# An attention front end with routed experts: the first group's v load put behind k, its queries turned early, the second group's loads issued early, the third group's casts in other buffers

## Chip, cores, metric

The kernel runs on one core of one Trainium2 chip. The metric is device time in microseconds (us) of one execution. Several executions are timed, in rounds that alternate with the kernel before on the same chip. A ratio is the mean time of one kernel's fast runs over the mean of the other's fast runs of the same rounds, so it is not quite the ratio of the medians quoted beside it. "Fast" leaves out the executions over 1.5% above the fastest of the same kernel.

## The reference

Attention in which a query sees only keys of its own hash bucket (six sign bits of a projection), then a gated mixture of eight experts over the result.

```python
q_bits = (einsum('bhsd,dk->bhsk', q, proj) > 0); k_bits = likewise with k
mask = q_bucket == k_bucket                      # buckets from the six bits
attn = softmax(where(mask, q @ k.T / sqrt(64), -1e9)) @ v   # B, H, S, D = 4, 8, 768, 64
x = attn, as 3072 x 512
P = exp(x @ w_gate), then 8 rounds of row and column normalisation
out = sum over 8 experts e of P[:, e] * (relu(x @ w1[e]) @ w2[e])
```

## The kernel before

The attention goes in 8 groups of four heads (two groups a batch). The code below is condensed, with cuts marked by `...`. A group has 24 "units" (4 heads x 6 key tiles). A unit is a pair of score matmuls `st` on TensorE, one `exp` on ScalarE, and six small `num` matmuls. While group n is computed, `prepare(n + 1)` runs in steps that are tied to units by `due`: transposes on VectorE (DVE), casts on GpSimd (POOL), hash matmuls `pr`, bits, and many small copies that SyncE (SP) issues. From the third group on, spare TensorE time goes to the first expert's matmuls (`hp`, `yp`), so TensorE is nearly full from there (busy for 10.00 of the 10 us from 70 to 80).

```python
    def fetch(n, what, eng=nc.gpsimd):       # k, q: 768 KB each, v: 4 x 192 KB
        ...
    def prepare(n):
        ...                                  # t16: casts of k and q
            if n == 0:
                if x == 0:
                    t16 = hpool.tile([P, FO, S], F16, tag="h", name="t16")
                t16s[name] = t16[:, 2 * x:2 * x + 2, :]
            else:
                t16s[name] = wk.tile([P, 2, S], F16, tag="t16", name="t16")
        ...
        lag = 2 if n > 2 else 1
        due = (4, 5, 8, 9, 12, 15) if n == 1 else (0, lag, 2 * lag, 3 * lag, 4 + 3 * lag, 7 + 3 * lag)
        yield due[0]; turn_qk("k", 0)        # transpose (DVE) and cast (POOL)
        yield due[1]; turn_qk("k", 1); stack("k", 0)      # copies by SP, two a head
        if n == 0:
            for c in range(2): hashed("k", c)             # PE, into PSUM tile pr
            bits("k")                                     # DVE, from pr
        if n: stack("k", 1); fetch(n + 1, "k")
        yield due[2]; turn_qk("q", 0)
        yield due[3]; turn_qk("q", 1); stack("q", 0)
        if n: stack("q", 1); fetch(n, "v")
        ...                                  # weight loads of 1 MB for n = 2, 3, 5, 6
        yield due[4]; ...                    # n == 0: hashed("q"), bits("q"); else all hashes and bits
        if n < 3:
            move_bits("k"); move_bits("q")   # head 0: bits straight to ks, qs
        put_bits()                           # all bits to DRAM (ds<-bt)
        ...
        yield due[5]
        ...                                  # get_bits of heads 1 to 3 from DRAM, rest of the stacks
        cast_v()                             # POOL: 2 casts, then 6 sums
        if n == 0:
            fetch(1, "kq")
    ...
    fetch(0, "kqv", nc.sync)
    pin(nc.scalar.activation(out=mark, in_=ones[:, 0:1], func=Act.Exp))
    for x in range(32):                      # warm-up matmuls
        if x == 10:
            for _ in prepare(0): pass
        pin(nc.tensor.matmul(warm, ident, vas[1]..., start=True, stop=True))
```

The softmax here doesn't subtract the row's maximum and nothing guards it: scores larger than these inputs give would overflow.

Of the kernel before, what the change touches and what calls it, by code (L numbers as in the profile page):

```python
# [20 lines left out]
def kernel(  # L21
# [11 lines left out]
    nc = tc.nc  # L33
# [28 lines left out]
    def pin(ins):  # L62
        tc.keep_in_program_order(ins)
        return ins
# [11 lines left out]
    mark = consts.tile([P, 1], F32)  # L76
# [270 lines left out]
    nat, grp = {}, {}  # L347

    def fetch(n, what, eng=nc.gpsimd):
        b, g = groups[n]  # L350
        for name, src in (("k", k), ("q", q)):
            if name in what:
                x = 12 if name == "k" else 15
                t = acc_flat[:, x * DD:(x + 3) * DD].rearrange("p (m d) -> p m d", d=D)
                pin(eng.dma_start(out=t, in_=src[b, g * HG:(g + 1) * HG].rearrange("h (r m) d -> (h r) m d", r=R)))
                nat[name, n] = t
        if "v" in what:
            t = lv.tile([P, HG, KT * D], F32, tag="v", name="v")
            vsrc = v[b, g * HG:(g + 1) * HG].rearrange("h (r m j) d -> m r h (j d)", r=R, m=M4)
            for m in range(M4):  # L360
                pin(eng.dma_start(out=t[R * m:R * (m + 1)], in_=vsrc[m]))
            nat["v", n] = t

    def prepare(n):
# [4 lines left out]
        for x, name in enumerate("kq"):  # L369
            trs[name] = acc_flat[:, (18 + 3 * x) * DD:(21 + 3 * x) * DD].rearrange("p (c t) -> p c t", c=2)  # L370
            d[name] = wk.tile([P, HG, S], F16, tag=name + "s", name=name + "s")
            if n == 0:
                if x == 0:
                    t16 = hpool.tile([P, FO, S], F16, tag="h", name="t16")
                t16s[name] = t16[:, 2 * x:2 * x + 2, :]
            else:
                t16s[name] = wk.tile([P, 2, S], F16, tag="t16", name="t16")
# [20 lines left out]
        def hashed(name, c):  # L398
            o = 64 * "kq".index(name)
            for x in range(2):  # L400
                pin(nc.tensor.matmul(d["pr"][o + 32 * x:o + 32 * (x + 1), 0:HT], pb[:, c].rearrange("p a r -> p (a r)"),  # L401
                                     trs[name][:, c, x * HT:(x + 1) * HT], start=(c == 0), stop=(c == 1)))

        def bits(name):
            if name == "k":
                d["bt"] = wk.tile([P, HT], F16, tag="bt", name="bt", bufs=1)
            bt, pr = d["bt"], d["pr"][:, 0:HT]
            if name == "k":
                pin(nc.vector.tensor_scalar(bt[0:64], pr[0:64], 0.0, 0.5, op0=Alu.is_gt, op1=Alu.subtract))
                pin(nc.vector.tensor_scalar(bt[0:64], bt[0:64], BIG, None, op0=Alu.mult))  # L410
            else:
                pin(nc.vector.tensor_scalar(bt[64:P], pr[64:P], 0.0, qoff[64:P, 0:1], op0=Alu.is_gt, op1=Alu.subtract))
# [15 lines left out]
        def cast_v():  # L428
            v32 = wk.tile([P, 2, 3, D], F32, tag="v32", name="v32", bufs=1)
            for i in range(2):  # L430
                hs = slice(2 * i, 2 * i + 2)
                pin(nc.gpsimd.tensor_copy(va[:, hs, :, 0:D],
                                          nat["v", n][:, hs, :].rearrange("p h (t d) -> p h t d", d=D)))
            for i in range(2):
                hs = slice(2 * i, 2 * i + 2)
                pin(nc.gpsimd.tensor_tensor(v32, va[:, hs, 0:3, 0:D], va[:, hs, 3:6, 0:D], op=Alu.add))
                pin(nc.gpsimd.tensor_tensor(v32[:, :, 0], v32[:, :, 0], v32[:, :, 1], op=Alu.add))
                pin(nc.gpsimd.tensor_tensor(vs[:, hs, 0:D], v32[:, :, 0], v32[:, :, 2], op=Alu.add))

        lag = 2 if n > 2 else 1  # L440
        due = (4, 5, 8, 9, 12, 15) if n == 1 else (0, lag, 2 * lag, 3 * lag, 4 + 3 * lag, 7 + 3 * lag)
        yield due[0]
        turn_qk("k", 0)
        yield due[1]
# [3 lines left out]
        if n == 0:  # L448
            for c in range(2):
                hashed("k", c)  # L450
            bits("k")
        if n:
            stack("k", 1)
            if n + 1 < len(groups):
# [17 lines left out]
        if n == 0:  # L472
            for c in range(2):
                hashed("q", c)
            bits("q")
        else:
            d["pr"] = ops.tile([P, 512], F32, tag="o", name="pr")
            for c in range(2):
                for name in "kq":
                    hashed(name, c)  # L480
                if c == 0 and n < 3:
                    yield due[4] + 1
            bits("k")
            bits("q")
# [25 lines left out]
        if n:  # L510
            get_bits("k", 3)
            get_bits("q", 3)
        cast_v()
        if n == 0:
            fetch(1, "kq")

    def scores(n, h, kt):
        d = grp[n]
# [89 lines left out]
        for _ in it:  # L608
            pass

    fetch(0, "kqv", nc.sync)
    pin(nc.scalar.activation(out=mark, in_=ones[:, 0:1], func=Act.Exp))
    warm = ops.tile([P, 512], F32, tag="o", name="warm")
    for x in range(32):
        if x == 10:
            for _ in prepare(0):
                pass
        pin(nc.tensor.matmul(warm, ident, vas[1].rearrange("p h t d -> p (h t d)")[:, 0:512],
                             start=True, stop=True))
# [8 lines left out]
    due = 0  # L628
    owed = 0.0
    for u in range(len(units) + 1):  # L630
        if u < len(units):
            n, h, kt = units[u]
            b, g = groups[n]
            i = u % per
            if i == 0:
                prep = prepare(n + 1) if n + 1 < len(groups) else iter(())
                due = 0
            while due is not None and due <= i:
                due = next(prep, None)
            if n == len(groups) - 1 and i == 2:  # L640
                for _ in quarters_of_w(1):
                    pass
                for _ in quarters_of_w2(1):
                    pass
            if u + 1 < len(units):
                pts[u + 1] = scores(*units[u + 1])
# [216 lines left out]
```

## Time and profile before

Median 784.56 us of three runs (783.94 to 786.2). The execution that was profiled took 786.34 us.

The page's second part, the whole span in 40 slices of about 20 us: busy tenths of TensorE (PE), and the clock that it was granted.

```profile
PE   6888999999999999999999999999999999999996
PEclk9997999999999999999999999999999999999999
```

TensorE is busy for 90% or more from the fifth slice on. The clock digit drops to 7 in the fourth (about 59 to 79 us). So most of what can be won without less matmul work lies in the first four slices. The timeline of TensorE there (start, duration, instruction, shape, count, and in brackets the idle time before it with what ended it):

```profile
13.15 4.92 PE L618 MATMUL warm<-va,ident 128*128 128x512 f16 x22
17.91 0.81 PE L521 MATMUL st<-qs,ks 71*128 71x384 f16 x4
...
59.32 0.66 PE L521 MATMUL st<-qs,ks 71*128 71x384 f16 x2 [1.14 <-ACT pt L524]
...
66.50 0.80 PE L521 MATMUL st<-qs,ks 71*128 71x384 f16 x2 [2.60 <-DMA qs<-ds]
69.74 1.44 PE L583 MATMUL hp<-xT,t 128*128 128x384 f16 x4 [0.30 <-ACT pexp L569]
...
76.14 0.81 PE L583 MATMUL hp<-xT,t 128*128 128x384 f16 x4
```

The first scores follow the warm-up matmuls at 17.91. At 66.50 TensorE has waited 2.60 us for the bits of the third group's second head. Four `hp` matmuls then take 1.44 us, later 0.81 (the last overlaps what follows). The stretches by window (start:end, length, busy us of PE, PEld, DVE, ACT, POOL with counts, granted clock, DMA share, GB/s) give the clock:

```profile
60.00:70.00 10.00, 6.73 (x94) 4.73 (x91) 5.67 (x10) 6.34 (x9) 5.75 (x10) 0.78 0.60 170
70.00:80.00 10.00, 10.00 (x77) 5.20 (x76) 4.68 (x10) 3.24 (x4) 4.20 (x7) 0.71 1.04 235
```

The chain of waits, followed back from the end of this part, runs through those bits (start, length, what):

```profile
55.69 5.88 DMA ds<-bt
61.91 4.45 DMA qs<-ds
66.50 0.80 PE st L521 x2
```

The put-bits copy to DRAM takes 5.88 us to land and the get-bits copy 4.45. ScalarE's timeline has the first exps:

```profile
18.43 8.73 ACT L524 ACTIVATE pt<-st 128x768 f16<-128x768 f32 x12 [16.14 <-DMA qs<-t]
```

| read from the timelines of this execution | us |
|---|---|
| first exp | 18.43 |
| 48 units at ScalarE's pace (0.73 us) | 35 |
| the same 48 units, from score pair to score pair | 41.4 |
| TensorE waits at units 24, 48, 54 | 1.04, 1.14, 2.60 |
| 60th exp (units counted from 0) | 80.07 |

### The profile page before, as it was taken

What the parts mean: (1) busy time and instruction counts of PE and PEld (TensorE: products, weight loads), DVE (VectorE), ACT (ScalarE), POOL (GpSimd) and SP (SyncE); (2) the same over time, 40 slices, a digit from 0 to 9 for tenths busy, and PEclk for the clock granted to TensorE, in tenths of its full rate; (3) what the DMA queues carried; (4) which work ended last, traced back from release to release, by engine and by line L of the source; (5) the groups of instructions that cost most, each with busy time, mean ns of one, the idle gap of its engine ahead of it and who ended that gap; (6) DMA issues with size and microseconds to landing.
All of it is one profiled execution on the core that took longest, in us unless ns stands there. A gap on an engine that the chain in (4) does not pass through costs nothing.

```text
span 784.6 us, 16637 instructions
## 1 busy us (share of the span) xinstructions
PE 751.7 (96%) x6252; PEld 518.2 (66%) x6252; DVE 558.1 (71%) x1240; ACT 507.7 (65%) x1020; POOL 312.6 (40%) x314
## 2 busy tenths in 40 slices
PE   6888999999999999999999999999999999999996
PEld 2554656666655667777777777777777777777663
DVE  3554757766758877777777777777777777777774
ACT  1894767777754777766666666666666666666660
POOL 6555355537600133344434334333444443324220
PEclk9997999999999999999999999999999999999999
DMA  5968467463003364486468647764874496443335
GB/s 151 252 153 203 118 168 156 143 156 89 2 1 55 54 108 81 83 160 108 82 110 158 109 81 131 129 118 82 147 121 92 92 168 108 81 82 81 81 82 135
DMA packets 42131, 88.56 MB, mean 113 GB/s; under 512 B 7426, under 2 KB 22402, under 8 KB 42050
## 3 DMA queue, kind: packets, MB, share of 16 engines
q0 software_dynamic: 27440, 71.06, 46.4%
q1 hardware_dynamic: 13718, 15.45, 7.5%
q10 hardware_dynamic: 892, 0.99, 0.5%
q8 instruction: 49, 0.80, 0.4%
q14 instruction: 32, 0.26, 0.1%
HBM read 53.07 MB, written 7.08 MB: 77 GB/s over the span
## 4 chain that ended last, share of the span: by engine, by line
PE 81%; DVE 5%; ACT 5%; DMA 3%; issue 2%; POOL 2%; SPq 2%; ACTq 0%; POOLq 0%; DVEq 0%
PE a L741 18%; PE a L249 17%; PE d L741 13%; PE y L249 9%; PE st L521 5%; PE d L249 4%; PE hp L583 4%; PE yp L593 3%; PE num L537 3%; ACT pt L524 2%; PE hp L322 1%; DMA ds<-bt 1%; ACT acc L240 1%; PE yp L306 1%; PE pr L401 1%
## 5 line engine op out<-in xcount | busy, mean ns | idle before, releaser
L750 DVE CUSTOM_DVE_ANT_0 hT<-d,u 128x384 f16<-128x384 f32 x336 | 185.1, 551 | 96.3 <-ACT u L746 95.6
L253 ACT ACTIVATE vt<-a,p 128x256 f32<-128x256 f32 x324 | 153.3, 473 | 149.2 <-PE a L249 148.9
L524 ACT ACTIVATE pt<-st 128x768 f16<-128x768 f32 x192 | 146.7, 809 | 69.2 <-PE st L521 52.4
L746 ACT COPY u<-a 128x384 f32<-128x384 f32 x336 | 160.9, 479 | 23.3 <-PE a L741 19.7
L288 POOL DMA_DIRECT2D acc<-vt x72 | 61.4, 852 | 267.9 <-ACT vt L253 112.4
L249 PEld LDWEIGHTS <-hT 128*128 128x128 f16 x1296 | 126.3, 97 | 50.7 <-DVE hT L750 1.1
L249 PE MATMUL a<-t,hs 128*128 128x256 f16 x972 | 145.8, 273 | 2.0 <-ACT vt L253 1.0
L249 PEld LDWEIGHTS <-hs 128*128 128x128 f16 x972 | 94.8, 98 | 38.3 <-issue 2.8
L741 PEld LDWEIGHTS <-t 128*128 128x128 f16 x896 | 87.7, 98 | 36.4 <-issue 0.6
L741 PE MATMUL d<-xd,t 128*128 128x384 f16 x448 | 109.4, 326 | 0.3 <-DVE hT L750 0.3
L741 PE MATMUL a<-xT,s 128*128 128x384 f16 x448 | 109.4, 326 | 0.1
L521 PE MATMUL st<-qs,ks 71*128 71x384 f16 x384 | 95.3, 329 | 10.7 <-ACT pt L524 5.6
L249 PE MATMUL y<-t,hT 128*128 128x256 f16 x648 | 97.1, 272 | 0.0
L257 DVE SCALAR_TENSOR_TENSOR acc<-y,p,acc 128x256 f32<-128x256 f32 x162 | 77.3, 477 | 11.4 <-PE y L249 11.4
L537 PEld LDWEIGHTS <-pt 128*128 128x128 f16 x1152 | 61.2, 98 | 27.3 <-issue 1.8
L741 PEld LDWEIGHTS <-s 128*128 128x128 f16 x672 | 65.5, 98 | 17.3 <-issue 2.3
L537 PE MATMUL num<-va,pt 128*128 128x65 f16 x1152 | 67.3, 195 | 0.6 <-ACT pt L524 0.6
L521 PEld LDWEIGHTS <-ks 71*128 71x128 f16 x384 | 33.8, 99 | 34.6 <-issue 17.2
L780 ACT ACTIVATE hT<-a 128x384 f16<-128x384 f32 x112 | 54.0, 483 | 1.8 <-PE a L741 1.7
L741 PE MATMUL a<-xd,s 128*128 128x384 f16 x224 | 54.3, 323 | 0.7 <-ACT u L746 0.6
L741 PE MATMUL d<-xT,t 128*128 128x384 f16 x224 | 54.7, 326 | 0.0
L741 PE MATMUL a<-xT,t 128*128 128x384 f16 x224 | 54.7, 326 | 0.0
(102 smaller groups left out, 969.7 us busy)
## 6 DMA issues: line engine op xcount, KB each, us to landing
acc<-vt POOLq DMA_DIRECT2D x72, 512.0 KB, 4.8
t<-in_moe_w_dram POOLq DMA_DIRECT2D x24, 512.0 KB, 7.3
acc<-in_k_dram POOLq DMA_DIRECT2D x7, 768.0 KB, 5.7
acc<-in_q_dram POOLq DMA_DIRECT2D x7, 768.0 KB, 12.4
v<-in_v_dram POOLq DMA_DIRECT2D x28, 192.0 KB, 5.5
out_dram<-acc SPq DMA_DIRECT2D x82, 64.0 KB
t<-in_moe_w_dram POOLq DMA_DIRECT2D x4, 1024.0 KB, 11.5
ks<-t SPq DMA_DIRECT2D x64, 48.0 KB
```

What stands on the lines that cost most here:

```text
L249: pin(nc.tensor.matmul(dst, hq[hn][:, fo, :], wq[wn][:, fo, :], start=first and fo == 0, stop=fo == FH - 1, skip_group_check=True))
L253: pin(nc.scalar.activation(out=vt[:, k], in_=a, func=Act.Copy, scale=p))
L257: pin(nc.vector.scalar_tensor_tensor(out=dst, in0=src, scalar=p, in1=dst, op0=Alu.mult, op1=Alu.add))
L288: pin(nc.gpsimd.dma_start(out=acc[:, b, i], in_=vt, accum_op=Alu.add))
L521: pin(nc.tensor.matmul(st[:, i, 0:HT], d["k"][0:KR, h, kt * P:(kt + 1) * P], d["q"][0:KR, h, i * HT:(i + 1) * HT], start=True, stop=True))
L524: pin(nc.scalar.activation(out=pt, in_=st[:, :, 0:HT], func=Act.Exp, scale=scale))
L537: pin(nc.tensor.matmul(num[:, j * (D + 1):(j + 1) * (D + 1)], pf[:, j * P:(j + 1) * P], va[:, h, kt, :], start=(kt == 0 and j == 0), stop= ...
L583: pin(nc.tensor.matmul(hp[:, 0:HT], w1[:, do, fo * P:(fo + 1) * P], xT[:, do, b * S + t * HT:b * S + (t + 1) * HT], start=(do == 0), stop= ...
L741: pin(nc.tensor.matmul(bk, wq[wn][:, do, f * P:(f + 1) * P], xq[xn][:, do, :], start=first and do == 0, stop=do == 1, skip_group_check=True))
L746: pin(nc.scalar.copy(t, bk))
L750: pin(add(TENSOR_ADD_SAT, out=dst, in0=bk, in1=u, s0=3e38, s1=0.0))
L780: pin(nc.scalar.activation(out=hT[:, f, hi], in_=a, func=Act.Relu))
```

## The change

The intent is a shorter front: let q arrive before v and turn it at once; fetch the second group's k and q before V's sums rather than after them, with its steps one or two units sooner; and free the third group from the two t16 buffers, which the second group's copies still read.

```diff
@@ prepare
-            if n == 0:
+            if n in (0, 2):                      # third group's casts in an h buffer
@@ cast_v
                 pin(nc.gpsimd.tensor_copy(va[:, hs, :, 0:D], ...))
+            if n == 0:
+                fetch(1, "kq")                   # between V's casts and V's sums
             for i in range(2): ...               # sums
@@ prepare
-        due = (4, 5, 8, 9, 12, 15) if n == 1 else ...
+        due = (3, 4, 7, 8, 10, 13) if n == 1 else ...
@@
             for c in range(2):
                 hashed("k", c)
-            bits("k")
@@
             for c in range(2):
                 hashed("q", c)
+            bits("k")                            # behind the queries' hash matmuls
             bits("q")
@@
         cast_v()
-        if n == 0:
-            fetch(1, "kq")
@@ start
-    fetch(0, "kqv", nc.sync)
+    fetch(0, "kq", nc.sync)
     pin(nc.scalar.activation(out=mark, in_=ones[:, 0:1], func=Act.Exp))
+    pin(nc.scalar.copy(mark, nat["k", 0][:, 0, 0:1]))    # waits for k
+    fetch(0, "v", nc.scalar)
```

More of the change, by code (lines that the diff above doesn't have):

```diff
@@ L440, in prepare @@
         lag = 2 if n > 2 else 1
-        due = (4, 5, 8, 9, 12, 15) if n == 1 else (0, lag, 2 * lag, 3 * lag, 4 + 3 * lag, 7 + 3 * lag)
+        due = (3, 4, 7, 8, 10, 13) if n == 1 else (0, lag, 2 * lag, 3 * lag, 4 + 3 * lag, 7 + 3 * lag)
         yield due[0]
```

## The prediction

> **What bounds the kernel now.** From about 76 us on, TensorE: the stretches by window show it 100% busy at full clock. No changed line touches that part; it can only begin sooner. What is left to win is the front:
>
> - 0 to 17.9 us, start: in the timeline the first score matmul (17.91) follows the last warm-up matmul (22 of them, 4.9 us, behind the queries' hash matmuls at 11.52 to 13.2).
> - 17.9 to 59.3 us, 48 score units: ScalarE's exp sets the pace, 0.73 us from start to start, 35 us for 48; they take 41.4. ScalarE's timeline shows 8.8 us of idle up to 67.4: 2.4 around 27 to 31 (third head's first unit, hash matmuls), 0.9 at 38.6 (a DMA), 1.3 at 45 to 48 (hash matmuls), 1.2 at 59 (third group's first head), 2.8 before 67.4 (third group's second head: TensorE waits 2.6 for the get-bits DMA).
> - 66.5 to 75.5 us: after that wait the clock is about half: four hp matmuls take 1.44 us instead of 0.65; granted clock 0.78 and 0.71 in 60:70 and 70:80. [...] I read this as about 4 us lost.
>
> **What the change moves.** It adds one small `mark` copy (0.2 us); v's four issues move from SP to ScalarE, idle then.
>
> 1. q no longer shares bandwidth with v, so its transposes (1.8 us) follow k's at 8.4 instead of 10.5; k's bits come 0.5 us later, q's 2 us sooner. The 22 warm-up matmuls then end near 16, and so does the wait for q's bits: 2 us saved. v should still land near 11, when GpSimd needs it.
> 2. The second group's k and q are issued near 13 instead of 18.5, so their transposes come at 19 to 22 instead of 23.7 to 29; with bits two units earlier this preparation gains 4 us (then limited by SP's issues, 0.6 to 0.7 us each). That takes most of the 24th unit's wait and 1 us of the 27 to 31 gap. Its 1.5 MB now meets the first group's small copies at 14 to 19: up to 1 us of new wait at the first group's second head.
> 3. The third group's casts no longer wait for the second group's copies out of the t16 buffers (k's 1.4 us at 43.8, q's at 49.1). Casts, bits and put-bits come 8 us sooner (put-bits now: issue 55.7, landing 5.9 later, then 4.5 for get-bits: the chain of waits from 45 to 66.5). The waits at 59 and 66.5 shrink to under 1 us together, and the cold clock goes.
>
> **Sum** (an estimate from these): 2.0 start, 1.3 at unit 12, 0.6 at unit 24, 1.0 and 2.4 in group three, 4.0 cold clock, less 1.0 of new waits: 10.3 us, all on the critical path, since what follows is TensorE bound. The ideal is about 15, so over 2% (15.7) is unlikely.
>
> Predicted 774.0 us, 80% range 770.0 to 780.0. Chances: faster by over 2% 0.05, within 2% 0.94, slower 0.01.
>
> **What would show it.** First score matmul near 16; the second group's k transposes before 20; no TensorE wait over 1.5 us between 17 and 66; granted clock 1.0 in 50 to 80; the gate matmuls (lg) at 60 to 62 instead of 68.6; from there equal timelines, shifted.
>
> **What would make it wrong.** The first group's bits through DRAM are delayed by the early loads (several us at unit 6); one remaining idle still drops the clock; SP's issues, not buffers, hold the third group; or the first unit still waits for q's bits near 17.5.

## The result, and the profile after

Median 783.7 us (783.4 to 783.73, 4 runs) against 784.25 for the kernel before (783.66 to 786.2, 4 runs); ratio 0.9988, 95% interval 0.997 to 1.0006. The change has no measurable effect. The prediction, 774.0 with a range of 770 to 780, was wrong.

The page's second part after the change:

```profile
PE   6999999999999999999999999999999999999996
PEclk9699999999999999999999999999999999999999
```

The clock is now full in the fourth slice and low in the second. The timeline of TensorE, the lines that answer to those of before:

```profile
8.83 2.40 PE L401 MATMUL pr<-acc,pb 128*32 128x384 f32 x16
11.17 4.92 PE L620 MATMUL warm<-va,ident 128*128 128x512 f16 x22
15.93 0.33 PE L521 MATMUL st<-qs,ks 71*128 71x384 f16 x1
20.75 1.12 PE L521 MATMUL st<-qs,ks 71*128 71x384 f16 x3 [4.50 <-DMA qs<-bt]
22.13 0.80 PE L521 MATMUL st<-qs,ks 71*128 71x384 f16 x2 [0.26 <-ACT pt L524]
...
69.61 0.81 PE L583 MATMUL hp<-xT,t 128*128 128x384 f16 x4 [0.30 <-ACT pexp L569]
```

The warm-up matmuls do end near 16, as predicted, and q, loaded without v beside it, does come sooner: VectorE's four transposes of k and q run from 6.43 to 10.23 without a gap, where q's two began at 10.50 before. But the second half of the first score pair waits 4.50 us for q's bits, and the matmuls after it run slow (a score pair 0.80 instead of 0.48). So the first exp comes at 21.27:

```profile
21.27 1.51 ACT L524 ACTIVATE pt<-st 128x768 f16<-128x768 f32 x2 [14.58 <-PE st L521]
```

At the other end, the wait of 2.60 us is gone and `hp` runs at full speed; it starts at 69.61, where it started at 69.74. The wait did not go because the bits come sooner. The third group's put-bits and the get-bits for the queries of its second head are issued 2.3 and 2.5 us later than before (55.69 and 61.91 there):

```profile
58.02 0.44 SPq L417 DMA_DIRECT2D ds<-bt  x1
64.36 0.42 SPq L420 DMA_DIRECT2D qs<-ds  x1
```

It went because the units come later: exp 48 is at 63.36, where it was at 60.08. The stretches by window:

```profile
20.00:30.00 10.00, 8.99 (x67) 5.51 (x67) 3.04 (x6) 7.18 (x9) 2.17 (x3) 0.52 0.61 169
30.00:40.00 10.00, 9.45 (x101) 5.24 (x99) 5.51 (x10) 7.20 (x10) 5.70 (x9) 0.80 0.81 167
60.00:70.00 10.00, 9.10 (x130) 6.43 (x129) 7.81 (x14) 9.52 (x14) 9.05 (x14) 1.00 0.76 200
```

The low clock has moved from 66 to 76 us forward to 20 to 34. The chain of waits at the start, and the issues by GpSimd and ScalarE just before (POOL's timeline, then ACT's), show what held the bits:

```profile
12.99 1.99 DMA ks<-bt
15.01 5.70 DMA qs<-bt
```

```profile
14.47 0.74 POOL L355 DMA_DIRECT2D acc<-in_k_dram  x1
15.20 0.57 POOL L355 DMA_DIRECT2D acc<-in_q_dram  x1
```

```profile
12.81 2.94 ACTq L426 DMA_DIRECT2D qs<-bt  x2
```

The second copy of q's bits (5.2 KB) goes out at 15.01, when the copy of k's bits has landed, and lands at 20.70. The second group's k and q (1.5 MB) were issued at 14.47 and 15.20. The DMA view of the 2 us from 16 to 18 (queue, packets, MB, share of the 16 engines) has one queue only, GpSimd's:

```profile
q0 software_dynamic: 95, 0.58, 88.1%
```

No packet of SP's or ScalarE's queue started in these 2 us, though both had copies out; from 19 to 21 they move again. In the second profile of this kernel the first score pair waits 5.44 us for the same bits.

### The profile page after: what moved, and what is told of

Read it like the earlier page. It is cut to its first block, busy times and chain, and to the rows that moved or that the text cites. A ratio compares the mean times of both kernels' runs of the same rounds, so it can differ in the third digit from the quotient of the medians.

```text
span 782.0 us, 16637 instructions
## 1 busy us (share of the span) xinstructions
PE 752.3 (96%) x6252; PEld 519.0 (66%) x6252; DVE 558.8 (71%) x1240; ACT 508.3 (65%) x1021; POOL 313.7 (40%) x314
## 4 chain that ended last, share of the span: by engine, by line
PE 83%; ACT 8%; DVE 5%; issue 2%; DMA 1%; POOL 0%; ACTq 0%; SPq 0%; DVEq 0%; POOLq 0%
PE a L743 18%; PE a L249 17%; PE d L743 13%; PE y L249 9%; PE st L521 6%; ACT pt L524 5%; PE d L249 4%; PE hp L583 4%; PE yp L593 3%; PE num L537 3%; PE pr L401 2%; ACT acc L240 1%; PE hp L322 1%; PE yp L306 1%; DVE hT L752 1%
## 5 line engine op out<-in xcount | busy, mean ns | idle before, releaser
L249 PEld LDWEIGHTS <-hs 128*128 128x128 f16 x972 | 94.8, 98 | 38.3 <-issue 2.8
L521 PE MATMUL st<-qs,ks 71*128 71x384 f16 x384 | 97.7, 336 | 9.0 <-DMA qs<-bt 4.5
L537 PE MATMUL num<-va,pt 128*128 128x65 f16 x1152 | 68.4, 196 | 0.6 <-ACT pt L524 0.6
```

The source lines that it names most:

```text
L249: pin(nc.tensor.matmul(dst, hq[hn][:, fo, :], wq[wn][:, fo, :], start=first and fo == 0, stop=fo == FH - 1, skip_group_check=True))
L521: pin(nc.tensor.matmul(st[:, i, 0:HT], d["k"][0:KR, h, kt * P:(kt + 1) * P], d["q"][0:KR, h, i * HT:(i + 1) * HT], start=True, stop=True))
L537: pin(nc.tensor.matmul(num[:, j * (D + 1):(j + 1) * (D + 1)], pf[:, j * P:(j + 1) * P], va[:, h, kt, :], start=(kt == 0 and j == 0), stop= ...
```

## The experiments

Unit times below are starts of the exps in ScalarE's timeline, counted from 0 (unit 24 begins group two, unit 48 group three, unit 54 its second head).

### First batch: undo or do one part

**e1_late_fetch**: the changed kernel with the early loads undone.

```diff
-            if n == 0: fetch(1, "kq")        # between casts and sums
         cast_v()
+        if n == 0: fetch(1, "kq")
```

> The changed kernel with one part undone: the second group's k and q loads go back behind V's sums (issue near 17.5 instead of 14.5). Theory A (these 1.5 MB hold up the small copies of the first group's q bits): the wait of 4.5 us before the first unit's second score matmul goes, the second unit's scores come near 16.5, the clock stays at 1.0 from 10 to 40, and the time falls to about 777 (774 to 780). Rival B (the bits are late because ScalarE's own queue now carries V's load ahead of them, and its issues are slow): the first exp stays near 21 and the time near 783.5.

**e2_early_fetch_alone**: the kernel before with that part alone.

```diff
+            if n == 0: fetch(1, "kq")        # between casts and sums
         cast_v()
-        if n == 0: fetch(1, "kq")
```

> The kernel before with one part alone: the second group's k and q loads between V's casts and V's sums (issue near 14.8). Theory A: the first exp moves from 18.4 to about 21, the clock is about half for the next 10 us, and the time is 2 to 5 us above the kernel before. Rival B: the first exp stays near 18.4, the second group comes earlier, and the time is equal or lower.

The waits of TensorE from 0 to 82 us (total, times, longest) in e1, then in e2:

```profile
PE st L521 <- DMA qs<-bt: 0.9, 1, 0.9
```

```profile
PE st L521 <- DMA qs<-bt: 2.7, 1, 2.7
```

On the wait, theory A holds: without the early loads 0.9 us instead of 4.5 and the first exp at 17.91 instead of 21.27; with them alone, a wait that the kernel before does not have, and the first exp at 22.32 instead of 18.43. On the time it fails. e1 took 782.57 us (779.12 to 785.86), ratio 0.9988 (0.9962 to 1.0015), where 777 was expected. e2 took 784.85, ratio 1.0018 (0.9997 to 1.004), although its first unit comes 3.9 us later. In e1 the clock fell all the same, from 20.6 to 30.8 in the trace's clock record, and a hash matmul group took 2.83 us at 27.04 (in the changed kernel 1.51, also at half clock, at 31.16). The loads are late there and the step is two units sooner; in e5, which has both too, TensorE waits 2.9 us at this step for the queries' transposes. So e1 is not a clean undoing; it pairs late loads with early steps. Its profiled execution, at 779.12 us, was the fastest of its six; 1.6 us of its lead over the first profile of before come from the part after unit 60 (see the last table), which no edit touched.

**e3_h_buffers_alone**: the kernel before with `if n in (0, 2)` alone.

> The kernel before with one part alone: the third group's casts into the h buffers. If buffers held up the third group (as predicted): its put-bits issue comes some 5 us sooner than 55.7, the TensorE wait of 2.6 us at 63.9 and the half clock after it go, and the time falls by 5 to 7 us to about 778. If SP's issues or the late transposes hold it, the wait stays and the time is within 1 us of before.

784.57 us (782.1 to 785.83), ratio 1.0009 (0.9986 to 1.0032): no gain. Put-bits of the third group in SP's timeline, before and in e3:

```profile
55.69 0.44 SPq L417 DMA_DIRECT2D ds<-bt  x1
```

```profile
57.45 0.44 SPq L417 DMA_DIRECT2D ds<-bt  x1
```

It is issued no sooner. The t16 buffers were a wait that GpSimd had (1.40 us before its cast at 43.76 in before, none before the one at 43.48 in e3), but they did not hold the third group. The half clock came at 42 to 49 here, after a wait of 2.0 us at unit 24.

**e4_bridge_warm**: the changed kernel with more warm-up matmuls.

```diff
-    for x in range(32):
+    for x in range(52):
```

> The changed kernel with 20 more warm-up matmuls (52 instead of 32), which keep TensorE busy up to about 20.2, where the first bits land at 20.7. It leaves the wait and takes only the idle time away. If the half clock after the idle time costs what I read (exps 0.97 instead of 0.73 us apart for 12 units, hash matmuls twice as long): clock 1.0 throughout, 4 us below the changed kernel, about 779.5. If the half clock costs nothing since other waits fill it: within 1 us of 783.7.

The clock stayed full at the start, and the first 24 units took 19.94 us (exp 0 at 20.86, exp 24 at 40.80) where the changed kernel took 23.04. That is the price of the half clock there: 3.1 us. The time did not follow: 785.27 (781.77 to 786.31), ratio 1.0016 (0.999 to 1.0041). The three microseconds were waited away at unit 48, in TensorE's timeline of e4:

```profile
62.65 0.82 PE L521 MATMUL st<-qs,ks 71*128 71x384 f16 x2 [3.42 <-DMA ks<-t]
```

The half clock came there, from 61.6 to 68.4 in the clock record.

### Second batch: keep TensorE busy, relieve SP

**e5_late_fetch_busy**: e1 with doubled score matmuls.

```diff
-        for i in range(2):
+        for i in ((0, 0, 1) if n < 2 or (n == 2 and h < 2) else range(2)):
```

By theory C the half clock is where the gain of e1 went.

> The changed kernel with late loads (e1_late_fetch) and, in units 0 to 59, the first of each pair of score matmuls done twice, to fill TensorE's idle time there (0.16 us of 0.73 a unit). Theory C ([...]that is where the gain of e1_late_fetch went): no half clock between 17 and 40, the 24th unit's exp 3 us sooner than 41.4, so near 38.3. A wait of 1 to 3 us at the 54th unit may then come up, since SP issues the third group's put-bits near 55 to 58 in every kernel so far; if it does, the half clock comes there and the time is near 781, if not, near 778. Rival D (the half clock costs nothing, the units wait for data anyway): the 24th unit stays near 41.4.

**e6_busy_no_sp_queue**: e5 with eight copies off SP.

```diff
-                pin(eng(name, h).dma_start(...))                                       # stack
+                pin((nc.gpsimd if n == 2 and h < 2 else eng(name, h)).dma_start(...))
```

> e5_late_fetch_busy, with the eight copies of the third group's first two heads (keys and queries) issued by GpSimd instead of SP. Theory E (SP's queue in its order, blocked by the wait for the second group's put-bits, holds up the third group, not the t16 buffers): put-bits of the third group is issued at 51 to 53 instead of 56 to 58, no wait over 1 us at units 48 and 54, no half clock up to 75, and the time is the lowest so far, about 776. Rival (late transposes or DMA bandwidth hold it): put-bits stays within 1 us of where e5_late_fetch_busy has it.

**e7_keys_bits_first**: e6 with the keys' bits ahead.

```diff
         if n == 0:
+            bits("k")
             for c in range(2): hashed("q", c)
-            bits("k")
             bits("q")
```

> e6_busy_no_sp_queue with the keys' bits taken right after the queries' transposes, ahead of the queries' hash matmuls. Theory: the keys' bits wait for the queries' hash matmuls (same PSUM tile), their copies go out 1.5 us later than in the kernel before, and the second copy of q's bits waits for them; with this the keys' bit copies are issued near 11.2 instead of 12.4, the second copy of q's bits near 14.1 instead of 15.0, and the first exp comes near 17.0 instead of 17.9; the time 1 us lower than e6_busy_no_sp_queue. If the first unit is held by something else, no change.

**e8_before_busy**: the control, doubled score matmuls in the kernel before.

> Control: the kernel before with the doubled score matmuls alone. Its wait of 2.6 us at the 54th unit stays, so the half clock after it stays too: time within 2 us of the kernel before, half clock from about 65 to 75. If the doubled matmuls alone brought a gain as large as in e5_late_fetch_busy, or a loss, the reading of that run would have to be corrected by it.

All four failed. The times were 786.04, 789.71, 787.67 and 788.06, with ratios of 1.0029, 1.0065, 1.0087 and 1.0039, every interval above 1. The doubled matmuls are a poor filler: 14 of the 24 executions still had a mean clock of 0.992 or less, down to 0.977 (the kernel before: down to 0.987), and at half clock a unit with three score matmuls asks more of TensorE than one with two (three took 1.14 us at 33.80 in e7, two 0.83 at 23.07 in the changed kernel). That the loss comes from this was not tested apart. The ratios carry outliers, too: two of e7's six executions took 796 us at a clock of 0.979, the other four 787.04 to 787.72. The profiled e8 kept a full clock until the last 1.3 us and took 782.35 us. One more execution of e8, at a mean clock of 0.998, took 783.75; the four at 0.991 and 0.992 took 787.82 to 788.76, 5.3 us more between the means. What can still be read: e5's unit 24 came at 43.93, not 38.3, since TensorE waited 2.9 us in the hash matmuls for the queries' transposes, the flaw of e1. Put-bits of the third group moved from 56.67 (e5) to 54.81 (e6), short of the 51 to 53 expected. e7's bits went out as expected (k's at 11.40), but the first exp stayed at 17.73: the queries' hash matmuls now wait 1.0 us for the keys' bits, which holds the warm-up matmuls back.

### Third batch: is the start on the critical path?

**e9_start_alone** and its repeat **e9b_start_alone**: the kernel before with the changes to the start alone (the moved `bits("k")` and the three lines under "start" in the diff above).

> The kernel before with the start's part of the change alone (v behind k on ScalarE's queue, the queries' transposes ahead of the keys' bits). Theory F (up to the 54th unit the kernel is held by the third group's preparation, a chain of issues on SP's queue with its put-bits at 55 to 58 in every kernel so far; a start that is sooner or later is waited away at units 48 and 54): first exp near 17.9 instead of 18.4, the 54th unit's exp still at 66 to 68, time within 1.5 us of before. Rival G (the start is on the critical path, as I predicted): the 54th unit's exp as much sooner as the first, and the time lower by that.

> Repeat of e9_start_alone for its profile. Theory F as there: first exp near 17.9, the 54th unit's exp at 65.5 to 69, no part of the sooner start left there.

e9's profiled execution is useless: 2716.56 us with no clock on record. Its five timed runs are normal: median of all six 784.46, ratio of the fast runs 1.0016 (0.9997 to 1.0035). In e9b's profile (784.07 us, one run) the first exp is at 17.77, but TensorE then waits 3.2 us at unit 12, unit 24 comes at 42.45 and unit 54 at 66.98, within the spread of the kernel before (66.47 and 67.40 in its two profiles). This run also shows what the start is worth without the early loads: its second copy of q's bits goes out at 15.2, where the kernel before has 15.3 (tile view of `bt`), so its first exp is only 0.7 us sooner than in the first profile of before, not 2.0.

**e12_start_held**: the kernel before, held back.

```diff
-    for x in range(32):
+    for x in range(46):
```

> The kernel before with 14 more warm-up matmuls (46 instead of 32), which hold the first unit back by about 3 us and do nothing else. Theory F: first exp near 21.4, but the waits at units 24 to 54 shrink by as much, the 54th unit's exp at 66.5 to 68.5 as before, the time within 1.5 us of before. Rival G: everything after comes 3 us later and the time is 3 us longer.

TensorE's timeline, the first scores and the wait that was left at unit 54:

```profile
21.86 0.81 PE L521 MATMUL st<-qs,ks 71*128 71x384 f16 x4
...
67.74 0.80 PE L521 MATMUL st<-qs,ks 71*128 71x384 f16 x2 [2.05 <-DMA qs<-ds]
```

This is the sharpest of the runs. The first exp came at 22.39, 4.0 us later than before; the time was 783.94 (782.25 to 786.72), ratio 1.0009 (0.9988 to 1.003), and the interval, which reaches up to 2.3 us, leaves out the 3 us (0.38%) that rival G asked for. Unit 54's exp was at 68.63, with a wait of 2.1 us still before it. A start that is 4 us later costs nothing that can be measured, so one that is sooner could hardly pay. One thing was not separated: the mean clock was 0.992 to 0.995 here and 0.989 to 0.994 in the kernel before, so less half clock may have paid for part of the delay. e2 has no such help (0.988 to 0.990); its first unit came 3.9 us later, and its interval, too, includes no change.

**e10_sp_relief_alone**: e3 with the eight copies issued by GpSimd (the edit of e6).

> The kernel before with the third group's casts in the h buffers and the eight copies of that group's first two heads issued by GpSimd instead of SP. Theory F: put-bits of the third group at 51 to 54 instead of 55.7 (57.5 in e3_h_buffers_alone), the 54th unit's exp at 62 to 65 instead of 66 to 68, the time 2 to 5 us below before. If the hash matmuls or DMA bandwidth hold that chain: put-bits stays at 55 to 58 and the time within 1.5 us.

784.86 us, ratio 1.0015 (0.9996 to 1.0033). Put-bits went out at 56.40, unit 54's exp came at 69.01, both outside what theory F asked for. SP's issue of those copies isn't the limit by itself. It may be a part of it: put-bits came 1.05 us sooner than in e3 (and 1.9 us sooner in e6 than in e5), in an execution that waited 3.2 us at unit 24 and had half clock from 39.2 to 49.5.

**e11_candidate**: e1 with `due` of the kernel before, the edit of e7 and the edit of e6.

> A candidate to beat both: the changed kernel with the second group's loads late, its steps at their old units, the keys' bits ahead of the queries' hash matmuls, and the third group's first eight copies issued by GpSimd; no doubled matmuls. If theory F and the half clock together are the whole story: first exp near 17.7, no TensorE wait over 0.9 us to unit 54, the 54th unit's exp at 61 to 64, no half clock, and the time near 777 (774 to 780). [...]

The run: 784.02 us (782.85 to 786.88), ratio 1.0016 (0.9997 to 1.0035): no gain. Put-bits came at 53.70 and unit 54 at 65.47, 1.9 us sooner than in the first profile of before, but waits were left: 1.7 us at unit 24, and 2.1 us in which TensorE waited for VectorE, which waited 3.5 us for the fourth group's q load. Half clock followed each (39.8 to 46.6, 70.5 to 73.9).

### Fourth batch: fill exactly the waits

Spare score matmuls, into the bank that the real ones then overwrite, ahead of the units that wait; the counts differ by kernel.

```diff
+        g0, h0 = (d, h - 1) if h else (grp.get(n - 1), HG - 1)
+        for _ in range({(1, 0, 0): 6, (2, 0, 0): 6, (2, 1, 0): 12}.get((n, h, kt), 0)):
+            pin(nc.tensor.matmul(st[:, 0, 0:HT], g0["k"][0:KR, h0, 0:P], g0["q"][0:KR, h0, 0:HT], ...))
```

**e13_before_bridged**, the kernel before with this:

> The kernel before with spare score matmuls (0.16 us each, into the bank that the real ones then overwrite) ahead of the units that wait: 6 at unit 24, 6 at unit 48, 12 at unit 54 (2.0 us of a wait of 2.6). They take up idle time and no more. If the half clock after the wait costs 3.4 us (exp 54 to exp 60 is 12.7 us in the kernel before and 9.2 in the others): no half clock between 60 and 76, exp 54 to exp 60 in 9.2 to 9.8 us, the time 2 to 3.5 us below before. If the half clock is not where the time goes: time within 1 us of before.

**e14_changed_bridged**, the changed kernel with this and the 52 warm-up matmuls of e4:

> The changed kernel with 20 more warm-up matmuls (e4_bridge_warm) and spare score matmuls ahead of unit 24 (6), unit 48 (12, 2.0 of the wait of 3.4 us there in e4_bridge_warm) and unit 54 (6). If the half clock is where the changed kernel's gain went: no half clock before the end, exp 54 near 68, gate matmuls near 69, time 2 to 4 us below e4_bridge_warm and 1 to 3 below before, near 781. Otherwise within 1 us of before.

**e15_candidate_bridged**, e11 with this:

> The candidate e11_candidate with spare score matmuls ahead of unit 24 (9, for its wait of 1.7 us), 48 (6) and 54 (6). Half clock at 40 to 47 gone, exp 54 at 62.5 to 64 instead of 65.5. Its second wait (TensorE 2.1 us for VectorE at 68.5 to 70.7, which waits for the fourth group's q load) stays or grows by what is gained before it, since that load's landing does not move: then gate matmuls 2 us sooner and the time at most 1 us better than e11_candidate, near 783. If that load moves too, near 780.

e13: 783.49 us (782.39 to 784.33), ratio 1.0002 (0.9984 to 1.002). In its profile the half clock after unit 54 is gone, but one came at 42.6 to 49.4 instead, after a wait of 1.1 us at unit 24. Three of its six runs had a mean clock of 0.997 to 0.999, so at most about 5 us of half clock in the whole execution (an estimate: 0.003 of 783 us, divided by 0.5). They took 782.39, 782.86 and 782.92; the three at 0.994 to 0.995 took 784.05 to 784.33. So the two sorts differ by 1.5 us here. e14: 785.78 (782.22 to 786.77), ratio 1.0027 (1.0003 to 1.0052), a little slower, although its profiled execution (783.34) had a full clock until the last 2.3 us and no TensorE wait over 0.72 us at a unit. Its other run at a high clock (0.997) took 782.22, and the four at 0.991 to 0.993 took 785.70 to 786.77, 3.4 us more between the means. So with hardly any half clock both kernels take 782.2 to 783.3 us, where the kernel before had a mean of 783.2 in these rounds (779.75 to 785.0): 0.5 us won, within its spread, and not the 4 of the prediction. e15: 784.37, ratio 1.0017 (0.9998 to 1.0036), the wait for VectorE still 1.7 us; the half clock at 40 to 47 went as expected, but another came at 28.9 to 32.3, and exp 54 was at 66.97, not at 62.5 to 64.

### Last: both kernels a second time

**before_again** and **after_again** are the two kernels, unedited.

> The kernel before, unchanged, profiled a second time. Theory H (the profiled execution was a slow one; the waits and the half clock fall elsewhere and cost less in the others): the profiled time is nearer 783.5, the half clock lies at another place or is shorter than 10 us, exp 60 comes 2 to 3 us sooner than 80.1, and the 2.6 us wait at unit 54 is not the same. If the first profile was typical: wait over 2 us at unit 54, half clock from about 65 to 76, exp 60 near 80.

> The changed kernel, unchanged, profiled a second time. If the early loads hold the first bits in every execution: first exp near 21, half clock from about 20 to 34, exp 60 near 77; the time equal to before within 0.3%.

before_again took 783.3 us (782.11 to 783.84) and after_again 784.38 (782.21 to 784.85), against 784.14 of the kernel before in the same rounds: ratios 0.9988 (0.9973 to 1.0003) and 0.9996 (0.9979 to 1.0012). The first compares the kernel before with itself, and 0.9988 is just what the change had scored.

TensorE's waits (0 to 82 us) in the second profile of before, which took 782.11 us:

```profile
PE st L521 <- ACT pt L524: 2.1, 8, 0.6
PE st L521 <- DMA ds<-bt: 1.6, 1, 1.6
PE st L521 <- DMA qs<-t: 0.6, 1, 0.6
```

The stretches by window of that execution:

```profile
40.00:50.00 10.00, 9.53 (x91) 5.70 (x92) 6.27 (x11) 6.55 (x9) 6.90 (x12) 0.66 0.39 124
60.00:70.00 10.00, 9.21 (x127) 6.51 (x127) 7.80 (x14) 8.68 (x13) 5.33 (x9) 1.00 0.46 143
70.00:80.00 10.00, 10.00 (x113) 6.12 (x112) 6.56 (x13) 6.20 (x9) 5.98 (x10) 1.00 1.05 245
```

The wait of 2.60 us for get-bits isn't there, the clock is full from 60 to 80, and a half clock of 6.8 us comes at 42 instead, after a wait of 1.6 us. The second profile of after repeats its first in the wait (total, times, longest), and its half clock lies at 20.7 to 34.4; exp 60 came at 78.22, a little later than expected:

```profile
PE st L521 <- DMA qs<-bt: 5.4, 1, 5.4
```

The four profiles side by side, in us:

| | before | before_again | after | after_again |
|---|---|---|---|---|
| first exp | 18.43 | 18.68 | 21.27 | 22.41 |
| exp 0 to 24 | 21.04 | 21.63 | 23.04 | 22.73 |
| exp 24 to 48 | 20.61 | 21.72 | 19.05 | 19.43 |
| exp 48 to 54 | 7.32 | 4.44 | 4.44 | 4.43 |
| exp 54 to 60 | 12.67 | 9.22 | 9.22 | 9.22 |
| exp 60 at | 80.07 | 75.69 | 77.02 | 78.22 |
| exp 60 to the end | 704.56 | 704.70 | 704.98 | 704.89 |

Against the first profile of before, the first profile of the change wins 3.1 us up to exp 60; against the second it loses 1.3. The last row is the same to 0.4 us: past unit 60 the change did nothing. That part isn't a constant, though. Over all 19 readable profiles it takes 702.6 to 706.1 us, and 703.0 or less in e1, e2 and e11. From 110 to 220 us TensorE waits 2.4 us for VectorE's `hT` in the first profile of before (waits view). So a part of the spread between executions may lie there.

## Why the prediction was wrong

In short, the sum took the waits and the half clock of one execution for the kernel's own, and added everything up as if all of it lay on the critical path. before_again lacks the two largest terms without any change, and in e12 a start 4.0 us later did not reach the end. Term by term:

- **What bounds the kernel** held in the main: the part from unit 60 on is equal in these four profiles to 0.4 us, and their differences arise before it. "100% busy" was read up to 100 us only; later TensorE has gaps (above).
- **"2.4 in group three, 4.0 cold clock"**, the two largest terms of the sum, failed first. They were read from one execution and taken for the kernel. In before_again the first is absent (exp 48 to 54 in 4.44 us) and so is the second (exp 54 to 60 in 9.22), without any change. Its own loss is a wait of 1.6 us and a half clock at unit 24. The profiled execution was 1.8 us above the median on the first page of numbers, and that was to be seen.
- **"2.0 start"** had the wrong sign: +2.8 and +3.7 us. The second copy of q's bits was issued only when k's had landed, at 15.01 instead of near 14 (by the chain of waits; in e7, with k's bits sooner, the two issues follow each other without a gap), since k's bits now come behind the queries' hash matmuls; and the early loads then kept them from landing until 20.70 (in e1, where these loads go out at 18.61, TensorE had the bits by 17.45). Without these loads the gain was 0.7 us (e9b), so the 2.0 was too large in any case: the kernel before issues that copy at 15.3, and the change, meant to win 2 us here, at 15.0.
- **"Less 1.0 of new waits ... at the first group's second head"** named the collision, but mis-sized and misplaced it: 4.5 and 5.4 us, at the first head's first unit, followed by a half clock of 13.7 us in both profiles, worth 3.1 us by e4. The fear was on the list of what could go wrong.
- **"1.3 at unit 12, 0.6 at unit 24"**: units 0 to 24 took 1.1 to 2.0 us longer, not 1.9 less, since this is where the half clock went. The second group's preparation did not gain 4 us either: its put-bits went out at 38.99 instead of 35.14. k's transposes came sooner (19.66 instead of 23.71), but q's later (30.12 instead of 27.35), because the steps are tied to units, and the units ran late; before q's, VectorE had waited 6.86 us for a matmul of the units (`mp`). The gain came after it: units 24 to 48 took 1.2 to 2.7 us less, pairing the least and the most favourable of the profiles.
- **"Casts no longer wait for the buffers, put-bits 8 us sooner"** failed. Put-bits came at 58.02 and 58.64, later than 55.69. e3 shows that freeing the buffers alone changes nothing; what else holds these casts was not singled out.
- **"All on the critical path"** failed: e12 moved the start by 4 us, and the time stood still. My reading: the front has several preparations running side by side (loads, put-bits and get-bits, the exps), and a gain in one is waited away in the next. e4 won 3.1 us by unit 24 and waited 3.4 at unit 48.
- **The clock**: that it falls around a wait was seen again (1.6 us in before_again, 4.5 in the changed kernel), and the price of a spell, 3.1 us of one front by e4, was near the 4 I gave it. That the change would take it away was not. The changed kernel has one at the start, the kernel before has one at 42 or at 66, and runs with hardly any (e13 and e14 at 0.997 and above) were only 0.5 us below before's mean.

What stays open: which preparation paces unit 54. Its exp lies between 65.3 and 70 in every kernel whose profile I can read without doubled matmuls, and put-bits of the third group goes out between 53.7 and 59.7. It is not the start (e12), not the buffers alone (e3), and not the buffers with SP's issue of the first eight copies (e10). e11 points at the loads, with the fourth group's q behind a 1 MB weight load (issued at 54.82 and 54.06; VectorE had q at 68.47), but no run took those loads away. That the front's slack absorbs a delay of the start is shown, and so that a sooner start can't pay much; the name of the last link isn't. No version beat the kernel before by more than its own spread.

## What to carry to other kernels

Before costing a change from waits and clock drops in one profile, set the profiled execution's time beside the median, and if the waits are 1 to 3 us, take a second profile: a kernel compared with itself gave 0.9988 here. Test with a delay whether a stage is critical at all, since holding it back costs one edit and answers for every speed-up of it. Don't release a large load in front of small copies that the next matmul waits for: here 1.5 MB so released went with a copy of 5.2 KB that took 5.70 us to land, and a wait of 4.50 us.

## What the runs show of the clock and the queues

- The clock fell around short waits: in before_again at 42.1 us, 2.4 us after the end of a single wait of 1.6 us; in the first profile of before at 65.6, 1.7 us into the wait of 2.60; in e1 at 20.6, after waits of 0.9 and 0.7. Not every such wait did it: 1.04 and 1.14 us in the first profile of before did not, nor did 1.83 in e2 (10.7 to 12.6) and 1.84 in e6 (26.6 to 28.4). So no limit comes out for the length of a wait, and what decides was not shown. The half-clock spells in the front were 3.4, 6.8, 10.2 and 13.7 us long.
- A spell cost less than its length: the first 24 units lost 3.1 us to one of 13.7 us (after against e4). At full clock ScalarE's exps set the pace there, 0.73 us a unit (before); at half clock a unit took 0.97 (after). Executions at a high and at a lower mean clock differed by 1.5 us (e13), 3.4 us (e14) and 5.3 us (e8, where doubled matmuls fill TensorE).
- From 16 to 18 us, 1.5 to 3.5 us after a load of 1.5 MB was begun on GpSimd's queue (14.47), no packet of SP's or ScalarE's queue started (95 packets, all of queue 0), and a copy of 5.2 KB that was out took 5.70 us to land (first profile of the change).
- Whole executions of one kernel differ: the kernel before ranged from 779.39 to 786.79 us, with the wait and the half clock at different units in its two profiles.
